# Early priorities of an attention-plus-FFN kernel taken from another replay, and its run-in products removed

## The chip, the cores and the metric

The kernel runs on one core of one Trainium2 chip. The metric is the device time of one execution in microseconds (us). Five engines work from their own instruction queues, each in its program's order: TensorE (PE; its weight loads are listed as PEld), VectorE (DVE), ScalarE (ACT), GpSimd (POOL) and SyncE (SP), which here only issues DMAs.

## The reference

Windowed attention on 8 batches of 8 heads, 576 positions, head size 64, then a Fourier mix over positions and channels, a normalisation and an FFN of 512 to 2048 to 512:

```python
scores = scale * np.matmul(q, k.transpose(0, 1, 3, 2))
# heads 0-3: the last 32 positions; heads 4-7: every 4th of the last 128
scores = np.where(masks[None], scores, -1e9)
attn = softmax(scores)
x = np.matmul(attn, v)                       # heads side by side: (8, 576, 512)
mixed = np.real(fft(fft(x, axis=1), axis=2))
u = x + mixed
un = (u - mean(u)) / np.sqrt(var(u) + 1e-06)
out = u + np.maximum(un @ w_ch1, 0.0) @ w_ch2
```

w_ch1 and w_ch2 come as 64-bit words, which the kernel turns into pairs of 32-bit halves itself.

## The kernel before

**Attention.** Each batch has two kinds of heads (`dil` 1 for the plain ones, 0 for the dilated), and each kind five slots `u`, four whole and one half; so a batch is ten calls of `attend`. A slot is a chain over four engines: 16 small score products on TensorE (8 for the half slot), a mask with a running extreme for each of four head pairs on VectorE (L838), an exponential for each on ScalarE (L844), one or two transpositions on TensorE (L849) and their copy on ScalarE (L854), 16 value products on TensorE (L860), then sums, reciprocals and scaling on VectorE (L877 to L886). The result of batch 0 goes by small DMAs of GpSimd (`dil` 1) and ScalarE (`dil` 0) into the tiles `x`; later batches go through DRAM.

**Behind it** come, per batch, the Fourier mix (L1105 to L1185), the normalisation, and "fills": products with the first six of 16 pieces of the weights (L1358, L1375). From about 540 us on, a main stage of products L1753 and L1863 takes all ten remaining pieces. The weights are loaded by `words_of` (DMA L1259, 512 KB a piece) and unpacked on ScalarE and VectorE (L1261 to L1279).

**What sets the order.** Every operation is given to a planner (`Plan.add`) with an engine, a cost and a priority. `Plan.run` replays the program with these costs, always takes the lowest priority that can start, and the instructions are emitted in that order; on the chip each engine goes through its own list strictly in order, waiting for semaphores. Two tables shift single operations: `MOVED` adds to the priority, `HELD` to the earliest time, each by kind of operation and turn ('k' and 'v' are the loads of keys, queries and values, 's' scores to exponentials, 'p' transpositions to scaling, 'o' stores, 'w' and 'W' weights, 'u' and 'd' the fills, the rest mix and normalisation). Costs and tables act only on the order: nothing on the chip waits for a planned time.

**Buffers.** Scores live in PSUM banks of the names mix and ff, or sc and sd, two of each. Four key tiles kb0 to kb3 serve all batches; kb2 and kb3 hold the keys of the first five slots, kb0 and kb1 those of the next five.

**The run-in.** In the first slot, `scores` issues `N_RUN_IN` = 32 products of a column of zeros (`kb[0]()[:, 0:WIN]`, cleared at L704) before its 16 real ones, into the bank that the real ones then overwrite.

## Time and profile before

| | us |
|---|---|
| median of three runs | 1008.23 (1007.9 to 1010.74) |
| the profiled execution | 1012.46 |
| its span, first to last instruction | 1010.4 |
| TensorE busy | 962.6 (95% of the span) |
| TensorE not busy in 0 to 50 us | 26.0 |
| the same in 50 to 600 us | 13.8 |

The span is what the profile divides up; 2.1 us of the execution lie outside it, and the execution was 4.2 us above the median. TensorE's busy time is a modelled figure, since its matmuls overlap, so a busy TensorE need not be a fast one; idle time is the safer reading.

### The profile page before, as it was taken

How to read it: one execution, taken by the hardware profiler on the slowest of the kernel's cores; microseconds unless marked ns; L12 is line 12 of the kernel's file. 1: busy time of each engine (PE TensorE's matmuls, PEld its weight loads, DVE VectorE, ACT ScalarE, POOL GpSimd, SP SyncE). 2: the span in 40 equal slices, each digit the busy share in tenths (PEclk: the TensorE clock that was granted, in tenths of full speed). 3: DMA queues.
4: the chain of work that ended last, by engine and by line, in shares of the span. 5: the costliest groups of instructions: out<-in, count | busy, mean ns of one | idle time of the engine just before them, and what ended most of it. 6: DMA issues, size and time to landing. Idle time of an engine off the chain costs nothing.

```text
span 1010.4 us, 29386 instructions
## 1 busy us (share of the span) xinstructions
PE 962.6 (95%) x11189; PEld 876.8 (87%) x11189; DVE 820.5 (81%) x2738; ACT 565.6 (56%) x1483; POOL 202.1 (20%) x277
## 2 busy tenths in 40 slices
PE   5499999998999999999999999999999999999997
PEld 4247788887888888998998999999999999999997
DVE  4699776867787889669888599898888888898877
ACT  3465645554456443335455565757576757575663
POOL 3301342635443436500001001000001000000011
PEclk7599999999999999999999999999999999999999
DMA  9767776768785555265888953332313131314031
GB/s 294 231 229 247 246 218 191 231 190 242 232 248 150 180 166 177 63 210 177 289 296 338 307 137 105 64 95 74 115 54 116 53 116 54 117 52 126 1 115 53
DMA packets 110101, 166.63 MB, mean 165 GB/s; under 512 B 13028, under 2 KB 51988, under 8 KB 109962
## 3 DMA queue, kind: packets, MB, share of 16 engines
q1 hardware_dynamic: 106044, 157.42, 50.1%
q0 software_dynamic: 2880, 6.43, 2.1%
q8 instruction: 88, 1.44, 0.6%
q10 hardware_dynamic: 1038, 0.92, 0.3%
q14 instruction: 51, 0.42, 0.1%
HBM read 110.42 MB, written 53.40 MB: 162 GB/s over the span
## 4 chain that ended last, share of the span: by engine, by line
PE 64%; DVE 8%; DMA 4%; ACT 2%; issue 1%; SPq 1%; POOL 0%; DVEq 0%; ACTq 0%; POOLq 0%
PE ff L1753 21%; PE sd L1863 6%; PE ff L1358 6%; PE mix L1863 6%; PE sc L1863 6%; PE ff L1375 5%; PE ff L1863 3%; PE sc L1375 3%; DMA ut<-us 3%; PE sd L1358 3%; PE mix L1170 2%; PE mix L1105 2%; DMA wt<-wst 1%; DVE ut L1506 1%; PE sc L828 1%
## 5 line engine op out<-in xcount | busy, mean ns | idle before, releaser
L1358 PE MATMUL ff<-ut,wa 128*128 128x256 f32 x936 | 128.5, 285 | 1.6 <-DVE h L1367 0.9
L1428 POOL DMA_INDIRECT ut<-us,flip_sb x20 | 24.9, 1246 | 512.1 <-DVE ut L1457 213.2
L1375 PE MATMUL ff<-wa,h 128*128 128x512 f32 x468 | 121.6, 401 | 1.0 <-DVE h L1367 1.0
L1358 PEld LDWEIGHTS ff<-ut,wa 128*128 128x128 f32 x936 | 116.7, 188 | 6.1 <-DVE h L1367 1.7
L844 ACT ACTIVATE pm<-pm,mx 128x64 f32<-128x64 f32 x288 | 79.6, 340 | 53.0 <-DVE mx L838 50.1
L1375 PEld LDWEIGHTS ff<-wa,h 128*128 128x128 f32 x468 | 83.4, 189 | 17.7 <-DVE h L1367 1.4
L1753 PE MATMUL ff<-xb,wa 128*128 128x256 f32 x540 | 75.8, 281 | 0.1
L1753 PE MATMUL ff<-xb,left_w 128*128 128x256 f32 x486 | 69.4, 282 | 1.2 <-ACT sb L1761 0.7
L1753 PEld LDWEIGHTS ff<-xb,wa 128*128 128x128 f32 x540 | 68.4, 188 | 0.4 <-ACT ut L1761 0.4
L1753 PE MATMUL ff<-xb,late_w 128*128 128x256 f32 x486 | 68.8, 280 | 0.0
L1777 ACT ACTIVATE h<-s 128x256 fp32r<-128x256 f32 x134 | 55.4, 417 | 20.6 <-DVE s L1793 16.0
L1753 PEld LDWEIGHTS ff<-xb,left_w 128*128 128x128 f32 x486 | 62.1, 188 | 2.4 <-ACT ut L1761 1.2
L1753 PEld LDWEIGHTS ff<-xb,late_w 128*128 128x128 f32 x486 | 61.8, 188 | 0.3 <-ACT s L1761 0.2
L1365 ACT ACTIVATE h<-ff 128x256 fp32r<-128x256 f32 x78 | 28.4, 382 | 46.7 <-PE ff L1358 46.1
L1753 PE MATMUL ff<-xb,right_w 128*128 128x256 f32 x378 | 52.6, 280 | 0.1
L1761 ACT COPY s<-ff 128x256 f32<-128x256 f32 x90 | 33.5, 372 | 32.4 <-PE ff L1753 31.5
L1753 PEld LDWEIGHTS ff<-xb,right_w 128*128 128x128 f32 x378 | 48.3, 189 | 0.7 <-ACT s L1761 0.3
L1506 DVE STREAM_TRANSPOSE ut<-ut 128x512 f32<-128x512 f32 (+1 forms) x40 | 39.2, 999 | 9.9 <-DMA ut<-us 9.9
L1358 PEld LDWEIGHTS sd<-ut,wa 128*128 128x128 f32 x360 | 44.2, 188 | 2.1 <-DVE h L1367 0.9
L1375 PE MATMUL sc<-wa,h 128*128 128x512 f32 x180 | 44.8, 392 | 0.9 <-ACT h L1365 0.5
L1358 PE MATMUL sd<-ut,wa 128*128 128x256 f32 x360 | 45.2, 280 | 0.1
L854 ACT COPY ptsb<-sc 128x256 f32<-128x256 f32 (+1 forms) x75 | 25.5, 350 | 34.9 <-PE sc L849 34.8
(311 smaller groups left out, 2642.3 us busy)
## 6 DMA issues: line engine op xcount, KB each, us to landing
vt<-in_v_dram SPq DMA_DIRECT2D x64, 260.0 KB
wst<-in_w_dram SPq DMA_DIRECT2D x20, 512.0 KB
wt<-wst SPq DMA_DIRECT2D x40, 256.0 KB
us<-uc SPq DMA_DIRECT2D x36, 257.0 KB
part<-row SPq DMA_DIRECT2D x36, 256.0 KB
ut<-part SPq DMA_DIRECT2D x36, 256.0 KB
kb<-in_k_dram SPq DMA_DIRECT2D x30, 288.0 KB
ut<-in_w_dram SPq DMA_DIRECT2D x12, 512.0 KB
```

Of the source, the lines that this page charges most:

```text
L844: add("ACT", 0.25, lambda i=i: nc.scalar.activation(out=pm()[:, i], in_=pm()[:, i], func=AF.Exp, bias=mx()[:, i:i + 1], scale=-1.0), ((mx, ...
L854: add("ACT", act(n), lambda: nc.scalar.copy(out=pt()[:, 0:n], in_=split[0]()[:, 2 * P:2 * P + n]), (split[0],), (pt,), prio)
L1105: nc.tensor.matmul(ps()[:, :NSP], lhsT=lt, rhs=tab, start=(m == 0 and n == 0), stop=(m == 2 and n == (0 if b == 0 else count - 1)),)
L1358: nc.tensor.matmul(z()[:, :n_tok], lhsT=wf()[:, a, kk], rhs=ut()[:, p, kk], start=(kk == 0 and n == 0), stop=(kk == KT - 1 and n == 2),)
L1365: add("ACT", act(n_tok) - 0.03, lambda: nc.scalar.activation(out=h()[:, 0, :n_tok], in_=z()[:, :n_tok], func=AF.Relu), (z,), ((h, 0),), prio)
L1375: nc.tensor.matmul(acc(), lhsT=h()[:, a, P * s:P * s + P], rhs=wf()[:, p], start=(first and n == 0), stop=(last and n == 2),)
L1428: add("POOL", 1.3, lambda: nc.gpsimd.indirect_dma_start(u(0, C + 2), None, us[idx // 4](), bass.IndirectOffsetOnAxis(ap=flip_sb()[:, 4 * k ...
L1506: nc.vector.transpose(out=o[back], in_=x[:, g])
L1753: nc.tensor.matmul(up_bank()[:, lo:lo + TOK1], lhsT=ap()[:, a, kk], rhs=xb()[:, j, p, kk], start=(start and k == 0), stop=(k == 5), skip_g ...
L1761: add("ACT", act(n), lambda: nc.scalar.copy(out=dst()[:, 0:n], in_=up_bank()[:, 0:n]), (up_bank, held), (dst,), SOON - 1, urgent=True)
L1777: add("ACT", act(TOK1), lambda: nc.scalar.activation(out=ap()[:, 0], in_=src(), func=AF.Relu if relu else AF.Copy), need, (k0,), prio)
L1863: nc.tensor.matmul(acc()[:, TOK1 * half:TOK1 * half + TOK1], lhsT=ap()[:, a, P * half:P * half + P], rhs=wap()[:, q_].rearrange("p k f -> ...
```

## The change

`N_RUN_IN` and the loop that issues the run-in go. The numbers in `MOVED` and `HELD` are replaced by others, found by a replay in which TensorE also waits for its blocks of instructions, which are fetched by DMA behind the loads that are already queued. The computation itself stays as it was. Lines shift by two to seven, so L828 before is L821 now, and so on.

```diff
 N_WARM0, N_WARM1 = 6, 5
-N_RUN_IN = 32
 NXT = 0
...
 MOVED = {
...
-    'k': [19.08, 58.34, 34.6, 63.03, 36.08, 15.45, 40.88, 7.29, 74.69, 49.57, 28.29, 44.49, 25.51, 20.01, 20.91,
...
+    'k': [59.87, 47.84, 49.03, -21.99, 61.44, 42.62, 47.77, 54.19, 103.48, 39.4, 6.16, 32.37, 76.92, 8.06, 16.38,
...
-        run_in = N_RUN_IN if first and u == FIRST_TURNED[0] else 0
-
         def scores():
-            for _ in range(run_in):
-                z = kb[0]()[:, 0:WIN]
-                nc.tensor.matmul(split[0]()[0:WIN, 0:WIN], lhsT=z, rhs=z, start=True, stop=True)
             for j, at, rows, c in tiles():
```

What that does to the order, at three places. First SyncE's list of loads from the start of the program, before and then now (kb are keys, tq queries, the numbers behind a kb tell which tile; kb_175 is kb2, kb_176 is kb3):

```order
L772 DMA kb_176<-in_k_dram 128x256
L694 DMA ident_sb<-in_ident_dram 128x128
L772 DMA kb_174<-in_k_dram 128x576
L787 DMA tq<-in_q_dram 128x256 x2
L772 DMA kb_176<-in_k_dram 128x192
L690 DMA mask_sb<-in_mask_dram 128x320
L772 DMA kb_175<-in_k_dram 128x256
L772 DMA kb_173<-in_k_dram 128x576
L772 DMA kb_176<-in_k_dram 128x128
L772 DMA kb_175<-in_k_dram 128x192
```

```order
L770 DMA kb_175<-in_k_dram 128x192
L688 DMA mask_sb<-in_mask_dram 128x320
L770 DMA kb_173<-in_k_dram 128x576
L770 DMA kb_176<-in_k_dram 128x128
L770 DMA kb_175<-in_k_dram 128x256
L785 DMA tq<-in_q_dram 128x256
L770 DMA kb_174<-in_k_dram 128x576
L785 DMA tq<-in_q_dram 128x256
L770 DMA kb_176<-in_k_dram 128x256
L770 DMA kb_176<-in_k_dram 128x192
```

The first slot needs the first 128 columns of kb2 (loaded from ScalarE's queue) and of kb3 and one tile of queries: they stood up to the tenth DMA (kb_176, 128x128), and now up to the sixth (the first tq).

Second ScalarE's first exponentials (L844, now L837) and copies (L854, now L847), before and then now:

```order
L844 ACTIVATE pm_351<-pm_351,mx_352 128x64 x4
L844 ACTIVATE pm_358<-pm_358,mx_359 128x64 x4
L854 COPY ptsb_379<-mix_279 128x256
L854 COPY ptsb_381<-sc_333 128x256
L844 ACTIVATE pm_450<-pm_450,mx_451 128x64 x4
```

```order
L837 ACTIVATE pm_291<-pm_291,mx_292 128x64 x4
L847 COPY ptsb_335<-mix_273 128x256
L837 ACTIVATE pm_330<-pm_330,mx_331 128x64 x4
L847 COPY ptsb_345<-sc_307 128x256
L837 ACTIVATE pm_418<-pm_418,mx_419 128x64 x4
```

The first slot's copy, which its value products need, no longer stands behind the second slot's exponentials.

Third SyncE's list where the first weights stand, before and then now (in_w is w_ch1 or w_ch2, and ut the tile that its words go to):

```order
L800 DMA vt<-in_v_dram 128x260
L787 DMA tq<-in_q_dram 128x640
L787 DMA tq<-in_q_dram 128x512
L800 DMA vt<-in_v_dram 128x520
L772 DMA kb_175<-in_k_dram 128x576
L1259 DMA ut<-in_w_dram 128x512 x4
L732 DMA row<-in_chn_dram 128x258
```

```order
L798 DMA vt<-in_v_dram 128x260
L785 DMA tq<-in_q_dram 128x640
L798 DMA vt<-in_v_dram 128x520
L785 DMA tq<-in_q_dram 128x512
L770 DMA kb_175<-in_k_dram 128x576
L1252 DMA ut<-in_w_dram 128x512 x4
L785 DMA tq<-in_q_dram 128x640
```

The load of kb2 and the four pieces of weights keep their places; a load of queries has come up behind them. On TensorE the order of slots, transpositions and value products stays nearly that of before (its list is 64 hardware products shorter). One thing moves there: the scores of the third to fifth slots, in before 32 products, then the second slot's value products, then the last 8, now stand in a row of 40.

## Rows read from the trace of the kernel before

**Rows 1.** The page, parts 1 and 2: busy time; 40 slices of 25 us.
```profile
PE 962.6 (95%) x11189; PEld 876.8 (87%) x11189; DVE 820.5 (81%) x2738; ACT 565.6 (56%) x1483; POOL 202.1 (20%) x277
...
PE   5499999998999999999999999999999999999997
...
PEclk7599999999999999999999999999999999999999
```

**Rows 2.** The page, part 3: queue, kind, packets, MB, share of the DMA engines.
```profile
q8 instruction: 88, 1.44, 0.6%
```

**Rows 3.** Stretches of 5 us: busy time and count per engine, TensorE clock, DMA.
```profile
10.00:15.00 5.00, 3.46 (x134) 2.62 (x135) 1.49 (x20) 2.64 (x10) 0.56 (x1) 0.54 1.05 374
15.00:20.00 5.00, 4.03 (x133) 2.47 (x122) 3.63 (x33) 3.46 (x13) 4.03 (x8) 0.50 0.93 298
20.00:25.00 5.00, 3.02 (x158) 2.48 (x157) 3.00 (x31) 2.52 (x10) 3.94 (x9) 0.50 0.98 333
25.00:30.00 5.00, 1.61 (x7) 1.11 (x7) 0.00 (x0) 0.00 (x0) 2.32 (x6) 0.50 0.98 344
```

**Rows 4.** The same view, stretches cut where TensorE waited for "issue".
```profile
15.60:22.90 7.30, 6.49 (x250) 4.76 (x250) 5.30 (x52) 3.98 (x16) 5.87 (x12) 0.50 0.96 314
22.90:28.30 5.40, 0.12 (x7) 0.00 (x0) 0.76 (x12) 2.00 (x9) 2.86 (x6) 0.50 0.97 351
...
28.30:117.40 89.10, 70.90 (x1379) 47.66 (x1380) 80.39 (x387) 52.51 (x150) 18.95 (x30) 0.85 0.73 233
```

**Rows 5.** TensorE's timeline: start, duration, operation [idle before, its releaser].
```profile
3.84 3.46 PE L823 MATMUL mix<-kb 128*32 128x32 f32 x64 [3.84 <-DVE tail_sb L722]
...
10.59 0.28 PE L828 MATMUL mix<-kb,tq 64*32 64x64 f32 x1 [3.01 <-DMA kb<-in_k_dram]
...
14.31 0.31 PE L828 MATMUL mix<-kb,tq 64*32 64x64 f32 x1
...
16.06 0.31 PE L828 MATMUL sc<-kb,tq 64*32 64x64 f32 x1 [0.62 <-issue]
...
20.59 0.31 PE L860 MATMUL mix<-vt,ptsb 64*32 64x65 f32 x1
...
28.39 0.42 PE L828 MATMUL ff<-kb,tq 64*32 64x64 f32 x2 [5.38 <-issue]
...
32.48 0.39 PE L828 MATMUL sc<-kb,tq 64*32 64x64 f32 x2 [1.25 <-DVE xt L886]
...
39.44 0.72 PE L849 MATMUL mix<-ident_sb,pm 128*128 128x128 f32 x2 [5.49 <-ACT pm L844]
```

**Rows 6.** DMA by queue: all in 20 to 26 us (two), instructions in 26 to 28.
```profile
q1 hardware_dynamic: 545, 1.90, 91.0%
q0 software_dynamic: 221, 0.12, 6.6%
...
q8 instruction: 1, 0.02, 3.1%
```

**Rows 7.** SyncE's DMA issues, 14 to 25 us: start, duration, count.
```profile
14.10 0.80 SPq L800 DMA_DIRECT2D vt<-in_v_dram  x1
17.25 0.33 SPq L772 DMA_DIRECT2D kb<-in_k_dram  x1
17.62 3.02 SPq L1259 DMA_DIRECT2D ut<-in_w_dram  x4
...
21.37 2.98 SPq L800 DMA_DIRECT2D vt<-in_v_dram  x4
```

**Rows 8.** ScalarE's own DMA issues in its timeline, two of the groups.
```profile
34.92 1.22 ACTq L935 DMA_DIRECT2D xt<-xt  x2
...
43.75 3.56 ACTq L935 DMA_DIRECT2D x<-xt  x4
```

**Rows 9.** TensorE's waits from 57 us to 1003: total, times, longest (us).
```profile
PE sc L828 <- DVE xt L886: 3.0, 7, 1.0
PE mix L1136 <- issue: 1.4, 1, 1.4
PE sc L860 <- issue: 1.4, 1, 1.4
```

## The prediction

> **What bounds the kernel now.** [...] A later gain of order alone has little room: the largest waits of TensorE from 57 us on are 3.0, 1.4 and 1.4 us in total [rows 9]. The early part decides, and there the timeline [rows 5] shows what a shift is made of. TensorE waits for keys until 10.59, stops for 0.62 us before 16.06 and for 5.38 us before 28.39 with no semaphore that held it ("issue"), and for 5.49 us before 39.44 for an exponential.

> **What the "issue" waits are.** The queue that the profile calls instruction moved 88 packets of 16 KB [rows 2]; TensorE has 22378 matmuls and weight loads [rows 1], so a packet holds 254 of them, 256 with its other instructions. Between the first stop and the second lie 250 + 250 of them, two packets, and between the second and the wait at 117 us 1379 + 1380, which is eleven [rows 4]. So TensorE stops at ends of blocks. No instruction packet moved between 20 and 26 us, while the loads took 91 and 6.6% of the DMA engines; one moved between 26 and 28, and TensorE went on at 28.39 [rows 5, 6]. The block was asked for when TensorE crossed into the block before it. Counted in the program's order (four instructions for an fp32 product, two for a transposition, one for each wait beyond an instruction's first) that is the first value product of the half slot, at 20.59 [rows 5]. Just before, SyncE had queued kb2 (288 KB) and four pieces of weights (512 KB each) from 17.25 to 20.64 [rows 7]: 2.39 MB, or 7.2 us at the 333 GB/s that moved then [rows 3]. From 20.59 to 28.39 are 7.8 us. So the block waited behind the loads, and 2.1 us of those 7.8 had work.

> **The change, part by part.** The sum goes by when the second score product of the dilated half, at 32.48 in before [rows 5], comes in the new order; the list behind it is the same.

> 1. *The run-in.* 64 hardware products, 3.84 to 7.30 [rows 5]. They end before the wait for keys that lasts to 10.59, so taking them away is worth 0. The clock was near half speed with them as well (0.54 over 10 to 15 us, then 0.50) [rows 3], so nothing that they warmed is lost: 0.

> 2. *The start.* The first slot's loads now end after 928 KB instead of 1536 KB, but the second slot's, which stand next on TensorE, still need about 1.6 MB, so they come at about 10.5. The gain is behind them: the first slot's exponentials are done by then and its copy no longer waits for the second slot's. So the value products and the scores of 14.31 [rows 5] can come up to 1.3 us earlier, at 13.0 (two copies and four exponentials off the chain). Bounds 0 and -1.3; I take -1.0, since the block of 40 needs a bank that the first slot gives back.

> 3. *The blocks.* Without the 128 instructions of the run-in every block ends 128 instructions of work later. Counted in the new order the ends fall in the third of 16 value products of the third slot, in the 25th of the 40 scores that opened the dilated half, and in the 12th of the 16 behind them. The first of these blocks is asked for at about 12.9, and the block before took 5.4 us (about 10.7, at the first scores, to 16.06 [rows 5]), so it is there at about 17.8; TensorE arrives at 16.7 and stops for 1.1 us, 0.5 more than in before. At 17.8 it asks for the next. SyncE's wait from 14.90 to 17.25 was for scores that read kb2 [rows 7]; these are done by 14.3 now, so kb2 and the weights are queued from about 15.0 to 18.3. By 17.8 kb2 and three pieces stand there, 1.87 MB, and some 0.8 MB of loads before them, less 0.83 MB moved at 298 GB/s [rows 3]: 1.84 MB, 5.5 us. With the 2.4 us from a packet's start to TensorE (26.0 to 28.39 [rows 5, 6]) the block is there at 25.7 to 26.1. TensorE has work to about 20.3, so it stops for some 5.6 us: the stop of 5.38 us is not removed but comes two microseconds sooner. Bounds: 0, if the block is asked for before the weights are queued, and 8, if kb2, all four and the 0.8 MB stand ahead undrained.

> [...]

> 4. *Up to 32.48.* In before the masks and the exponentials ran during the stop, so 4.1 us lay between 28.39 and 32.48. In the new order the stop comes inside the 40 scores, and VectorE starts with masks of the part that is cut: ten masks and ten exponentials lie behind it, some 5.6 us to the second score product. That gives 26.1 + 5.6 = 31.7, so -0.8 in place of 32.48, between -2.9 and +2.0.

> 5. *From there to 50 us.* The wait that ends at 39.44 is for exponentials behind four DMA issues on ScalarE (the last two end at 36.14), and four more take 3.56 us from 43.75 [rows 8]. They have the same places in the new list, as has the unpacking of weights on VectorE around them: 0, so the -0.8 is carried on. From 50 us TensorE is full, so a shift is kept to the end.

> 6. *Later blocks.* The ends move in the same way against all later work. Two "issue" waits of 1.4 us [rows 9] are what such a stop costs there. They can go, and others can come: between -2.8 and +2.8, and I take 0.

> Sum: 0 - 0.8 + 0 + 0 = -0.8 us. The span would be 1009.6 instead of 1010.4. The profiled execution was 1012.46 and the median of the runs 1008.23; the 0.8 us are taken from the median: **1007.4 us**. A measurement of this kernel can tell about 0.3% from no change, 3.0 us, so this is "no change" in effect.

> **Rivals.** *A, the block is in time.* If TensorE crosses into the block before the weights are queued, the new order has no stop of five microseconds. For it: the change's numbers come from a replay that counts this wait, and TensorE would only have to be there 1.5 to 2.5 us sooner than I reckon. Against it: SyncE is ahead too, because its wait of 2.35 us is gone [rows 7]. The price is the 5.4 us, less what the loads of values behind the weights (21.37 to 24.35 [rows 7]) then hold back: 1002.8 to 1005.0, middle 1003.9. The same time follows if a block need not stand behind the loads at all. [...]

> *B, two stops for one.* The place is the next block, in the 12th of 16 scores, which is asked for when the first stop ends. If that is later than 28.4, it stands behind queries and values queued meanwhile (some 1.36 MB, 4.1 us, and 2.4), is there at 35.1 or later, and the second score product, which starts at 32.48 in before [rows 5], comes 2.6 us late. With 0.6 us of exponentials behind it this is +3.2 or more: 1011.4 to 1013. For it: all four pieces of weights are on the way earlier than before. Against it: 28.4 needs 2.3 us more of queue than 1.84 MB make.

> *C, the forecast*: the stop moves and stays, 1005.2 to 1011.2.

> **How the numbers follow.** C 0.58, A 0.29, B 0.13: the counted places of the blocks speak for C, and the largest doubt is whether 17.8 us is right within two microseconds, more likely early than late. Faster by over 0.3% is A, slower B. The likeliest gives 1007.4; its own range is 1005.2 to 1009.7 by items 2 to 6. The range reaches down to 1002.3, below A's middle by what item 6 can add to it, and up to 1010.8, which leaves out B and a quarter of A.

> **What would show it.** Right: a wait for "issue" of 4 to 7 us on TensorE that ends at 25 to 27 us, inside scores of the 40; one of about 1 us that ends near 17.8; the second scores at 31 to 32.5; TensorE full from about 50 us on. Wrong: no such wait (A), one that ends past 28.4 and another behind it (B), or a gain that comes after 57 us, which no term here has.

## The result, and the profile after

The changed kernel takes 1016.0 us (median of 20 runs, 1012.84 to 1021.26), the kernel before 1010.04 in 20 runs beside them (1007.9 to 1013.24). The ratio is 1.0059, with a 95% interval of 1.0048 to 1.0070: about 6 us slower, where 1007.4 and "no change" were forecast. The profiled execution of after was 1015.23, its span 1013.4, against 1012.46 and 1010.4: the two traces show 3 of the 6 us, since that execution of before lies above its median and that of after below.

The page of after, parts 1 and 2 (TensorE's busy time; 40 slices of 25 us), answers to [rows 1]:

```profile
PE 962.9 (95%) x11125; PEld 875.7 (86%) x11125; DVE 822.1 (81%) x2738; ACT 567.0 (56%) x1483; POOL 205.6 (20%) x277
...
PE   4499999999999999999999999999999999999997
...
PEclk9998999999999999999999999999999999999999
```

At this grain after looks no worse than before: nine tenths or more from 50 us on except the last slice. The first two digits of PEclk can't be compared with those of [rows 1], as shown below. The early part, in TensorE's timeline (start, duration, operation [idle before, its releaser]), answers to [rows 5]:

```profile
13.03 0.31 PE L853 MATMUL mix<-vt,ptsb 64*32 64x65 f32 x1
...
18.91 0.31 PE L853 MATMUL mix<-vt,ptsb 64*32 64x65 f32 x1 [0.92 <-issue]
...
24.95 0.31 PE L821 MATMUL sc<-kb,tq 64*32 64x64 f32 x1 [2.78 <-issue]
...
31.25 0.39 PE L821 MATMUL sc<-kb,tq 64*32 64x64 f32 x2 [1.26 <-DVE xt L879]
...
37.87 0.71 PE L842 MATMUL mix<-ident_sb,pm 128*128 128x128 f32 x2 [5.75 <-ACT pm L837]
```

Two stops at block ends, the second inside the scores of the 40 as counted, but 2.78 us long and not 5.6; the second score product of the dilated half comes at 31.25, 1.2 us sooner than the 32.48 of [rows 5].

The clock was half in the early part, as in [rows 3], although PEclk reads 9 there. The trace of after holds no record of the clock before the rise to full at 54.8 us, and a stretch without a record is counted as full. The products tell it (groups of score products: count | busy, mean ns of one; before in 20 to 50 us, where half is on record, then after in 20 to 50 and in 60 to 80 us):

```profile
L828 PE MATMUL sd<-kb,tq 64*32 64x64 f32 x72 | 3.2, 308 | 0.1
L821 PE MATMUL sd<-kb,tq 64*32 64x64 f32 x72 | 3.4, 309 | 0.0
L821 PE MATMUL sd<-kb,tq 64*32 64x64 f32 x56 | 1.8, 222 | 0.0
```

One product takes 309 ns in after where before takes 308 at half clock, and 222 behind the rise. Later the clock of after fell once more (stretches in us: length, busy time and count of PE, PEld, DVE, ACT, POOL, granted clock as a share of full speed, DMA share, GB/s):

```profile
82.00:90.00 8.00, 7.58 (x121) 6.19 (x121) 6.80 (x38) 3.84 (x12) 0.00 (x0) 0.57 0.82 253
90.00:100.00 10.00, 9.53 (x219) 8.47 (x218) 9.71 (x49) 7.37 (x20) 1.63 (x3) 1.00 0.64 215
```

**Where the time went.** I lined the two traces up by equal amounts of TensorE work, which is an estimate, since the order differs. After is 1.5 us ahead at 57 us, 3.7 ahead at 338 us, 2.0 ahead at 487, 0.8 behind at 596 and 3.2 behind at 677. The gain is there and is lost again between 370 and 680 us. Part of the gain is that both later "issue" waits of 1.4 us [rows 9] are gone from after's trace. The same view in two of these stretches, before and then after:

```profile
370.00:410.00 40.00, 39.32 (x263) 35.79 (x261) 34.35 (x81) 15.25 (x39) 23.84 (x29) 1.00 0.44 136
510.00:620.00 110.00, 108.83 (x811) 102.58 (x810) 89.63 (x207) 64.42 (x155) 6.33 (x3) 1.00 0.77 252
```

```profile
370.00:410.00 40.00, 37.54 (x244) 33.69 (x243) 30.42 (x72) 15.54 (x40) 19.56 (x25) 1.00 0.43 136
510.00:620.00 110.00, 105.75 (x790) 99.83 (x789) 87.08 (x201) 62.59 (x150) 8.40 (x3) 1.00 0.77 247
```

TensorE is idle for 2.46 us of the first stretch instead of 0.68, and for 4.25 of the second instead of 1.17: 4.9 us more, of the 6.9 that it falls back between 338 and 677. Its timeline of after names the waits:

```profile
387.18 4.37 PE L1351 MATMUL ff<-ut,wa 128*128 128x256 f32 x36 [1.78 <-DVE h L1360]
...
522.40 1.68 PE L1351 MATMUL sd<-ut,wa 128*128 128x256 f32 x12 [0.83 <-DVE h L1360]
...
550.86 1.65 PE L1746 MATMUL ff<-xb,right_w 128*128 128x256 f32 x12 [1.63 <-ACT ut L1754]
...
578.23 0.74 PE L1856 MATMUL sd<-late_w,row 128*128 128x256 f32 x4 [0.82 <-DVE row L1777]
```

The tables shift every kind of operation, the fills ('u', 'd'), the weights ('w', 'W') and the main stage's loads too, so the late order is new as well. In the first place VectorE has unpackings of weights (L1307, L1272) ahead of the awaited `h` (its timeline in after):

```profile
381.71 2.73 DVE L1307 TENSOR_TENSOR wst<-wst 128x256 f32<-128x256 f32 x3
384.37 0.41 DVE L1272 TENSOR_TENSOR right_w<-wst,right_w 128x256 fp32r<-128x256 f32 x1
384.70 0.41 DVE L1307 TENSOR_TENSOR wst<-wst 128x256 f32<-128x256 f32 x1
385.04 1.75 DVE L1272 TENSOR_TENSOR right_w<-wst,right_w 128x256 fp32r<-128x256 f32 x5
386.72 0.41 DVE L1360 SCALAR_TENSOR_TENSOR h<-ff,h 128x256 fp32r<-128x256 f32 x1
```

Ten operations in a row stand ahead of `h`, 5.1 us from the first's start to the last's end. In the second place it is ScalarE's copy `ut` that stands behind casts of weights, which wait for their DMA (its timeline in after):

```profile
548.61 0.41 ACT L1333 CAST wst<-wst 128x256 fp32r<-128x256 f32 x1 [3.14 <-DMA wt<-wst]
549.26 0.40 ACT L1333 CAST wst<-wst 128x256 fp32r<-128x256 f32 x1 [0.24 <-DMA wt<-wst]
549.92 0.40 ACT L1333 CAST wst<-wst 128x256 fp32r<-128x256 f32 x1 [0.26 <-DMA wt<-wst]
550.23 0.58 ACT L1754 COPY ut<-ff 128x512 f32<-128x512 f32 x1
```

The theory that I took to the chip: the loss is the late order's, made of these waits. Its rivals: the early part or the missing run-in costs time that the two single traces hide; or these waits are only where a shortage of supply shows, and go next door when removed.

### The profile page after: what moved, and what is told of

The parts are those of the page before. It is cut to its first block, busy times and chain, and to the rows that moved or that the text cites. A ratio compares the mean times of both kernels' runs of the same rounds, so it can differ in the third digit from the quotient of the medians.

```text
span 1013.4 us, 29258 instructions
## 1 busy us (share of the span) xinstructions
PE 962.9 (95%) x11125; PEld 875.7 (86%) x11125; DVE 822.1 (81%) x2738; ACT 567.0 (56%) x1483; POOL 205.6 (20%) x277
## 3 DMA queue, kind: packets, MB, share of 16 engines
q8 instruction: 88, 1.44, 0.6%
## 4 chain that ended last, share of the span: by engine, by line
PE 45%; DVE 11%; DMA 6%; issue 2%; ACT 1%; SPq 1%; DVEq 0%; ACTq 0%
PE ff L1746 19%; PE sd L1856 5%; PE sc L1856 5%; PE mix L1856 5%; DMA ut<-us 4%; PE ff L1856 3%; PE ff L1351 2%; PE ff L1368 2%; DVE ut L1499 1%; DVE wst L1307 1%; PE sd L1351 1%; DVE h L1360 1%; PE sc L1368 1%; SPq L1489 1%; DVE wst L1264 1%
## 5 line engine op out<-in xcount | busy, mean ns | idle before, releaser
L1421 POOL DMA_INDIRECT ut<-us,flip_sb x20 | 28.0, 1400 | 515.3 <-DVE ut L1450 201.9
L837 ACT ACTIVATE pm<-pm,mx 128x64 f32<-128x64 f32 x288 | 79.3, 339 | 49.2 <-DVE mx L831 46.3
L1770 ACT ACTIVATE h<-s 128x256 fp32r<-128x256 f32 x134 | 55.1, 416 | 22.8 <-DVE s L1786 18.3
L847 ACT COPY ptsb<-sc 128x256 f32<-128x256 f32 (+1 forms) x75 | 25.6, 351 | 36.5 <-PE sc L842 36.4
```

The costliest lines, as they stand in the source:

```text
L837: add("ACT", 0.25, lambda i=i: nc.scalar.activation(out=pm()[:, i], in_=pm()[:, i], func=AF.Exp, bias=mx()[:, i:i + 1], scale=-1.0), ((mx, ...
L847: add("ACT", act(n), lambda: nc.scalar.copy(out=pt()[:, 0:n], in_=split[0]()[:, 2 * P:2 * P + n]), (split[0],), (pt,), prio)
L1421: add("POOL", 1.3, lambda: nc.gpsimd.indirect_dma_start(u(0, C + 2), None, us[idx // 4](), bass.IndirectOffsetOnAxis(ap=flip_sb()[:, 4 * k ...
L1770: add("ACT", act(TOK1), lambda: nc.scalar.activation(out=ap()[:, 0], in_=src(), func=AF.Relu if relu else AF.Copy), need, (k0,), prio)
```

## The experiments

The kernels e1 to e11, g2 and g3, but for e3, hold both pairs of tables and replay the plan with each; what is emitted is one order up to a planned time and then what is left of the other, in its order. e3 and e12 are the kernels before and after, e3 without the run-in, and f1 to g1 move single operations in the order of after. A planned time is about 10 us below that of the chip (a cut at 330 lies near 340 us). Every comparison has its own runs of before beside it, whose medians lay between 1010.9 and 1012.7 us; so kernels are compared by their ratio to before, in brackets its 95% interval. These ratios are the ones on record; they are not the quotient of the two medians given with them, from which they differ by up to 1.7 thousandths (e7).

### Early or late, run-in or not

**e1: the new order to 340 us, the old one behind.**

```diff
-N_RUN_IN = 32
+N_RUN_IN = 0
+FIRST_PART, CUT = 0, 330.0
...
-        for o in order:
-            o.fn()
+        (one, at), (two, _) = self.replay(FIRST_PART), self.replay(1 - FIRST_PART)
+        early = {o.num for o in one if at[o.num] < cut}
+        for o in [o for o in one if o.num in early] + [o for o in two if o.num not in early]:
+            o.fn()
```

> The new order up to about 360 us (330 us of the planner's own clock), the old order behind it, no run-in. In the two traces the new order is 4.0 us ahead at 330 us and 3.0 us behind at the end, so 7 us are lost in between, and nothing before. Theory 'late' (the new order of fills and weight unpacking from 375 to 680 us makes TensorE wait): the loss goes and the lead stays, 4 us under before, about 1006. Theory 'run-in' (without the 64 products the clock or the ends of the instruction blocks fall worse): as the changed kernel, about 1016. Theory 'early' (in a typical run the new early order is the slow part): about 1016.

1012.38 against 1012.64: 1.0003 [0.9981, 1.0025]. The early part alone shows neither loss nor gain; with the late order the loss is gone. In its trace the two stretches are as in before:

```profile
370.00:410.00 40.00, 39.33 (x263) 35.81 (x262) 33.17 (x80) 15.13 (x39) 22.74 (x29) 1.00 0.42 136
510.00:620.00 110.00, 108.91 (x813) 102.75 (x812) 89.57 (x208) 64.27 (x154) 7.08 (x3) 1.00 0.79 252
```

**e2: the reverse, with the run-in and the old order to 340 us, the new one behind.**

```diff
-FIRST_PART, CUT = 0, 330.0
+FIRST_PART, CUT = 1, 330.0
```

> The other way round: run-in and old order up to about 360 us, the new order behind it. Theory 'late': 7 us over before, about 1017, with waits of TensorE for VectorE's half of h near 387 us and for ScalarE's copies near 550 and 577 us. Theories 'run-in' and 'early': as before, about 1010.

1017.56: 1.0050 [1.0019, 1.0082], with waits of 1.55 us at 391.59 and of 2.04 at 555.45 at the same two instructions as in after. The late order alone makes nearly the whole loss.

**e3: before without its run-in.**

```diff
-N_RUN_IN = 32
+N_RUN_IN = 0
```

> The kernel before with the run-in alone taken out; its order is the same to the instruction otherwise. Theory 'late': within 2 us of before (1008 to 1012), since the products end before the wait for keys; the ends of the instruction blocks move by 128 instructions, so the stop of 5.4 us before 28.4 us should move. Theory 'run-in': about 1016. Theory 'early': about 1010.

1016.55: 1.0029 [1.0008, 1.0051], so slower, which the prediction's item 1 had at 0. The blocks end elsewhere in the old order too (TensorE's timeline):

```profile
21.82 0.31 PE L860 MATMUL mix<-vt,ptsb 64*32 64x65 f32 x1 [2.59 <-issue]
...
28.13 0.31 PE L828 MATMUL sc<-kb,tq 64*32 64x64 f32 x1 [3.06 <-issue]
...
34.47 0.39 PE L828 MATMUL sc<-kb,tq 64*32 64x64 f32 x2 [1.28 <-DVE xt L886]
```

Stops of 2.59 and 3.06 us stand for 0.62 and 5.38 [rows 5], in sum no more than these, and the second score product is 2 us later. One of these two comes with the first keys, at 11.55 instead of 10.59, which differs from run to run (11.70 in e8, where they stand in the same place of the list). The profiled execution, 1019.14, is the slowest of e3's twelve, and its trace differs in the clock too: it rises to full at 59.3 us (54.7 in before) and falls to half again for 6.8 us at 86.6 and, by a wait of 2.31 us for `h`, at 253.9; the trace of before has no such fall. What makes the loss of e3 is open.

**e4: after with the run-in.**

```diff
-N_RUN_IN = 0
+N_RUN_IN = 32
```

> The changed kernel with the run-in put back; its order is the same to the instruction otherwise. Theory 'late': within 2 us of the changed kernel (1014 to 1018). Theory 'run-in': about 1010. Theory 'early': about 1016.

1015.02: 1.0034 [1.0009, 1.0059]. One stop of 3.96 us, ending at 26.94, stands for after's two, and the late waits stay (1.51 us at 389.26, 1.45 at 551.86). Its interval and that of the change overlap, so the run-in has no worth of its own here that these runs show.

### Which late stretch, and do the weights hold the block

**e5: the change with the old order in the two stretches.**

```diff
+PARTS = (('new', 360.0), ('old', 400.0), ('new', 500.0), ('old', 600.0), ('new', 100000000.0), ('new', 1000000000.0))
```

> The changed kernel with the old order in two stretches only (360 to 400 and 500 to 600 us of the planner's clock, about 10 us later on the chip), the new order everywhere else. In the new order VectorE has ten unpackings in a row ahead of the h that TensorE waits for at 387 us (1.78 us), and ScalarE three casts, which wait for stores of weights, ahead of the copy that gives back TensorE's bank at 550 us (1.63 us); in the old order these stand apart. Theory 'two places' (these and the waits beside them at 522 and 577 us make the loss): the waits go and the time falls by 3.4 to 6 us from 1016, to 1010 to 1012.6. Rival 'symptom' (TensorE is ahead there of loads and stores that set the pace, and what is mended comes back at the next wait): within 1 us of 1016, with other waits of the same sum up to 680 us.

1015.23 against 1010.92: 1.0040 [1.0019, 1.0062]. Both waits are gone from its trace (idle 0.67 and 2.35 us in the two stretches, span 1010.8; that execution, 1012.97, was 2.3 us under e5's median), but the ratio gives back only a third of the loss, less than the sum of the waits, and its interval and that of the change overlap.

**e6 and e8: e1, and before, with the third and fourth piece of weights behind four loads of values on SyncE.** They ask whether a block waits for the bytes queued ahead of it.

```diff
+LATER = (((('w', 2), ('w', 3)), ('v', 9)),)
```

> The new order up to about 340 us and the old one behind it, as in the first experiment, with one change: SyncE issues the third and fourth piece of weights (2 of the first 4, 512 KB each) behind the four loads of values that follow them. Theory 'behind the loads' (a block of TensorE's instructions is fetched only when the loads already queued have passed): 1.05 MB less stand ahead of it, 3.1 us at 335 GB/s, so the stop of 3.4 us at 23 us shrinks to under 1 us; the time falls by up to 3 us if nothing else is late, to 1009 to 1011. Rival 'own cost' (fetching a block at this place costs what it costs): a stop of 3 us stays and the time is that of the first experiment, 1012.

> The kernel before with the same two pieces of weights issued behind the four loads of values, nothing else changed. Theory 'behind the loads': the stop of 5.4 us before 28.4 us shrinks by about 3 us, and the second scores of the dilated half start near 29.5 instead of 32.5 us; the time falls by 1 to 3 us. Rival 'own cost': the stop stays over 5 us and the time within 1 us of before.

e6 1013.77: 1.0017 [0.9994, 1.0039]. e8 1010.42: 0.9989 [0.9968, 1.0011]. The stop in e1, e6 and e8, in that order:

```profile
26.32 0.31 PE L941 MATMUL sc<-kb,tq 64*32 64x64 f32 x1 [3.07 <-issue]
```

```profile
25.38 0.31 PE L963 MATMUL sc<-kb,tq 64*32 64x64 f32 x1 [3.88 <-issue]
```

```profile
27.14 0.42 PE L963 MATMUL ff<-kb,tq 64*32 64x64 f32 x2 [3.35 <-issue]
```

With two pieces (1.05 MB) behind the loads of values, e6's stop did not shrink (3.07 to 3.88), while e8's did (5.38 to 3.35). When TensorE crossed into the block before, the queue held 1.74, 2.25, 1.77, 1.57 and 1.25 MB in before, after, e1, e6 and e8 (bytes that SyncE had begun to issue, less those whose packets had started); so e6, which crosses 1.7 us sooner than e1, had only 0.2 MB less ahead. From the crossing to the packet were 5.45, 3.79, 3.81, 4.38 and 2.66 us, in which 1.67, 1.44, 1.36, 1.27 and 0.85 MB left that queue. The waits do not follow the bytes, and in after the packet moved with 0.8 MB still waiting. So a queue that holds the block strictly behind all bytes ahead of it, as the prediction and the replay have it, is refuted; what does set the wait stays open. And 2 us off the largest early stop show no gain clear of noise in e8's ratio, whose interval still holds one of that size.

**e7: e1 with the run-in.**

```diff
-N_RUN_IN = 0
+N_RUN_IN = 32
```

> The first experiment's order with the run-in of 32 products put back, so that the ends of the instruction blocks lie 128 instructions earlier. Theory 'ends of blocks' (the run-in only shifts the ends, which in this order cost 1.6 + 3.4 us without it and 4.2 us in one stop with it): 1 to 2.5 us less than without the run-in, 1010 to 1011.5. Rival 'nothing in it': the first experiment's 1012.4 within 1 us. Rival 'clock' (the run-in lets the clock fall to half from 10 to 55 us, which costs): over 1013.

1013.13: 1.0005 [0.9984, 1.0027], as e1. With the new early order the run-in is worth nothing that these runs show, with the old one its removal cost 2.9 thousandths (e3).

### The stretches again, by exclusion

**e9: the new order to 610 us. e10: new to 340 us and in the two stretches, old elsewhere. e11: new to 370 and from 410 to 510 us, old elsewhere. e12: the changed kernel once more, for its ratio in the same comparison.**

```diff
+PARTS = (('new', 600.0), ('old', 100000000.0), ('old', 1000000000.0))
...
+PARTS = (('new', 330.0), ('old', 360.0), ('new', 400.0), ('old', 500.0), ('new', 600.0), ('old', 100000000.0), ('old', 1000000000.0))
...
+PARTS = (('new', 360.0), ('old', 400.0), ('new', 500.0), ('old', 100000000.0), ('old', 1000000000.0))
```

> The new order up to about 610 us (600 of the planner's clock), the old order behind it, no run-in. The new order lost 5.6 thousandths behind 340 us; the old order in the two stretches gave back only about 2 of these in the median, though in its one trace the loss was gone. Theory 'two stretches' (the loss lies between 370 and 610 us): as the changed kernel, 5 to 6 us over before. Theory 'end' (the rest lies behind 610 us): 2 to 4 us over before.

> The new order up to 340 us, and again from 370 to 410 and from 510 to 610 us; the old order in all the rest, no run-in. Theory 'two stretches': they alone cost what the changed kernel costs, 5 to 6 us over before, with the waits of 1.8 us near 387 and near 550 us in the trace. Theory 'end', or a loss spread over other places: 1 to 3 us over before.

> The new order up to 370 us and from 410 to 510 us, the old order in the rest, no run-in; beside the kernel with the old order in the two stretches, the part behind 610 us is old too. Theory 'two stretches': within 1.5 us of before. Theory 'end': within 1.5 us of before as well, but then 3 to 4 us under the kernel whose end was new. A loss between 410 and 510 us, the only part behind 370 us that is new here: 3 us or more over before.

> The changed kernel itself once more, beside these on the same chip: 5 to 7 us over before by its first 20 runs (5.9 thousandths, 4.8 to 7.0). It also gives a second trace: theory 'order' has the waits near 387 and near 550 us again at 1.8 and 1.6 us, and a chance event would not come twice.

Against 1011.92: e9 1018.29, 1.0065 [1.0043, 1.0086]; e10 1019.59, 1.0073 [1.0045, 1.0101]; e11 1013.9, 1.0024 [1.0004, 1.0043]; e12 1016.45, 1.0058 [1.0033, 1.0083]. e12 confirms the change's ratio, and its trace has the two waits again, 1.89 us for `h` at 389.34 and 1.87 for `ut` at 553.03. e10 is e1 with the new order in two stretches of some 40 and 100 us, and with these the whole loss is back; what comes behind 610 us has no part in it that shows. But e5, without them, keeps two thirds of it: the stretches are enough for the loss, and not shown to be all of it. Its stretches:

```profile
370.00:410.00 40.00, 37.87 (x250) 34.25 (x249) 34.22 (x80) 14.69 (x37) 23.57 (x30) 1.00 0.43 136
510.00:620.00 110.00, 106.49 (x785) 100.25 (x784) 88.05 (x204) 64.61 (x154) 7.31 (x2) 1.00 0.79 253
```

TensorE's idle time in them (length less PE busy, us), for before, the change and the kernels so far that mix the orders or, as e4, have the new one throughout:

| | early part | 370 to 410 | 510 to 620 | ratio to before |
|---|---|---|---|---|
| before | old | 0.68 | 1.17 | 1 |
| e1 | new | 0.67, old order | 1.09, old order | 1.0003 |
| e11 | new | 0.68, old | 1.66, old | 1.0024 |
| e4 | new, run-in | 2.18, new | 1.98, new | 1.0034 |
| e5 | new | 0.67, old | 2.35, old | 1.0040 |
| e2 | old | 2.23, new | 4.04, new | 1.0050 |
| e12 | new | 2.56, new | 4.25, new | 1.0058 |
| after | new | 2.46, new | 4.25, new | 1.0059 |
| e9 | new | 2.95, new | 3.77, new | 1.0065 |
| e10 | new | 2.13, new | 3.51, new | 1.0073 |

The old order in the stretches goes with the lower ratios, the new one with the higher, and e4 and e5 cross. e5 and e11 have the old order in the stretches and pieces of the new one around them; their intervals reach down to 1.0019 and 1.0004, so a seam or a remainder may cost something there that was not found. No run prices a seam by itself, so e10's 1.0073 can hold the price of its seams as well.

### Is it the operations ahead of the awaited one

**f1: the change with the three casts behind the copy `ut`. f2: with the unpackings (the ten, and one behind the first `h`) and four casts spread behind the next four `h`. f3: both.** Numbers are those of the operations: each is emitted behind its mark, as far as its users allow.

```diff
+BEHIND = ((4432, 4493), (4435, 4499), (4438, 4504))
...
+BEHIND = ((4113, 3099), (4115, 3099), (4114, 3099), (4118, 3105), (4116, 3105), (4120, 3105), (4124, 3105), (4126, 3111), (4122, 3111), (4128, 3117), ...
```

> The changed kernel, and on ScalarE the three casts ahead of the copy at 550 us moved behind it, each behind one later operation, with their partners on VectorE; every other list is word for word the same. Theory 'list': the wait of TensorE of 1.6 to 1.9 us for that copy goes and does not come back, so the time falls by 1.5 to 2 us from 1016. Rival 'store' (what the casts wait for, the stores of weights, is what is late, and TensorE meets it at its next use): the wait stands at a place a little later, 1016.

> The changed kernel, and the ten unpackings in a row on VectorE ahead of the h near 387 us spread behind this h and the next three, as are the four casts on ScalarE that stand ahead of the activation for it; every other list is the same. Theory 'list': the wait of 1.8 us goes, 1.5 to 2 us less than 1016. Rival 'VectorE is full there': the wait goes to the next h, 1016.

> Both of these moves at once, nothing else. Theory 'list': 3.3 to 3.9 us less than 1016, and what is left over before (about 2 us) is made of the smaller waits near 522, 577 and 609 us. Rivals as in the other two: 1016.

Against 1012.74: f1 1019.66, 1.0076 [1.0048, 1.0103]; f2 1019.07, 1.0064 [1.0041, 1.0088]; f3 1019.48, 1.0079 [1.0052, 1.0106]. None gains. f1's wait at 550 is gone, and another stands 17 us behind it (TensorE's timeline, then ScalarE's):

```profile
568.19 0.98 PE L1896 MATMUL ff<-xb,left_w 128*128 128x256 f32 x6 [2.39 <-ACT sb L1904]
```

```profile
565.90 0.42 ACT L1920 ACTIVATE row<-s 128x256 fp32r<-128x256 f32 x1 [2.78 <-DMA part<-row]
567.25 0.42 ACT L1920 ACTIVATE row<-ut 128x256 fp32r<-128x256 f32 x1 [0.93 <-DMA part<-row]
567.57 0.57 ACT L1904 COPY sb<-ff 128x512 f32<-128x512 f32 x1
```

The copy `sb` now stands behind two operations that wait for stores of rows, which SyncE has among its loads of weights. In f3 the wait at 387 falls into 0.90 and 0.33:

```profile
393.64 1.65 PE L1501 MATMUL ff<-ut,wa 128*128 128x256 f32 x12 [0.90 <-DVE h L1510]
395.62 3.70 PE L1518 MATMUL ff<-wa,h 128*128 128x512 f32 x15 [0.33 <-DVE h L1510]
```

and the stretch is still idle for 2.06 us (2.46 in after). So the operations right ahead are not the cause by themselves. What differs is how much VectorE has to do while TensorE runs one row of 60 products; its groups in that row, in before (386.7 to 394.5 us) and then in after (382.3 to 391.6; line, engine, operation, count | busy, mean ns | idle):

```profile
L1314 DVE TENSOR_TENSOR wst<-wst 128x256 f32<-128x256 f32 x3 | 1.2, 409 | 0.0
L1279 DVE TENSOR_TENSOR right_w<-wst,right_w 128x256 fp32r<-128x256 f32 x5 | 1.8, 410 | 0.0
```

```profile
L1307 DVE TENSOR_TENSOR wst<-wst 128x256 f32<-128x256 f32 x4 | 3.1, 825 | 0.0
L1272 DVE TENSOR_TENSOR right_w<-wst,right_w 128x256 fp32r<-128x256 f32 x7 | 2.6, 411 | 0.0
```

Eight unpackings, 3.0 us, in before; eleven, 5.7 us, in after, of which three took 0.91 us each. f3, which spread them, still has nine in that row. That fits the first stretch; that it is the cause is argued from these counts, which lie close together, and not shown by an edit.

**g1: f1 with the stores of rows ahead of the weights on SyncE. g2: the change with the old order in the first stretch alone. g3: in the second alone.**

```diff
-BEHIND = ((4432, 4493), (4435, 4499), (4438, 4504))
+BEHIND = ((4432, 4493), (4435, 4499), (4438, 4504), (4075, 4074), (4077, 4076), (4442, 4076), (4443, 4076), (4444, 4076))
...
+PARTS = (('new', 360.0), ('old', 400.0), ('new', 100000000.0), ('new', 1000000000.0))
...
+PARTS = (('new', 500.0), ('old', 600.0), ('new', 100000000.0), ('new', 1000000000.0))
```

> The kernel with the three casts behind the copy, and on SyncE the two stores of rows (part) ahead of the last store of weights and of the first three loads of late_w; all other lists the same. With the casts moved the wait of 1.6 us at 550 us had gone, but a wait of 2.4 us for ScalarE's copy of sb stood near 568, behind an activation that waited 2.5 us for the store of a row, which stood in SyncE's list behind stores and loads of weights that were themselves waiting. Theory 'SyncE's list': that wait goes and the time is 2 us under that kernel's 1.0076 of before, near 1.0055. Rival 'supply' (the weights' stores, later by the moved casts, hold TensorE somewhere anyway): another wait of 1 to 2.5 us up to 620 us, 1.007 or more.

> The changed kernel with the old order between 370 and 410 us only. If the two stretches add up, this gives back what the traces show there, 1.8 to 2 us: 3.5 to 4.5 us over before. If TensorE waits in the second stretch for something that comes at its own time, the lead is lost there: 5 us or more over before.

> The changed kernel with the old order between 510 and 610 us only. If the two stretches add up, 2 to 3 us over before (the first stretch's 2 us stay, the 3 to 4 us of the second go). If the loss hangs on the first stretch (what comes late there comes late in the second as well): 5 us or more over before.

Against 1012.23: g1 1021.21, 1.0092 [1.0059, 1.0124]; g2 1017.08, 1.0052 [1.0034, 1.0069]; g3 1017.72, 1.0057 [1.0037, 1.0078]. g1's wait at 568 is gone, and a new one stands near 580 (its waits from 560 to 620 us: total, times, longest):

```profile
PE sd L2006 <- ACT row L1920: 2.0, 1, 2.0
```

f1 and then g1 moved the second stretch's wait to the next operation that needs weights or rows. So it is not the place of one operation; that the supply through SyncE is late there fits both, but no run changed the supply alone, and it stays open. TensorE is idle for 0.68 and 2.53 us in g2's two stretches, and for 2.99 and 2.57 in g3's: the old order mends the first stretch wholly, the second in part, and the new one left the second at 2.53 this time. Yet both ratios barely differ from after's 1.0059 (e12: 1.0058), and g2's traced waits are near those of e5 at 1.0040: the two stretches do not simply add, and the waits of one trace do not price a kernel within 2 us.

## Why the prediction was wrong

**What held.** The steps to 57 us, by after's rows above. *Item 2:* the scores that began at 14.31 came at 13.46, -0.85 for the -1.0 taken, with the first value product at 13.03 (13.88 in before). *Item 3:* two stops at the counted places, of 0.92 us (forecast 1.1) ending at 18.91 (17.8), and one that ends at 24.95, a microsecond before the 25.7 to 26.1 forecast. Its length was mis-sized: 2.78 and not 5.6, because TensorE arrived two microseconds later than reckoned and the packet came sooner than the queue allows: 3.79 us from the crossing, for the 5.5 reckoned from 1.84 MB, with 2.25 MB there. The rule behind item 3, that a block waits behind all bytes queued, is refuted by that. It had looked right in before because the 2.39 MB were taken as all still there, when 1.74 were. By the prediction's own sign, a wait of 4 to 7 us, the stop failed. *Item 4:* 31.25, so -1.2 for the forecast -0.8. That is near by luck: the stop ended a microsecond early, and 6.3 us instead of 5.6 lay behind it. *Item 5, to 50 us:* 37.87 against 39.44, carried on, 1.5 us ahead at 57.

**What failed.** First, "A later gain of order alone has little room", from which I concluded that "The early part decides". [rows 9] shows the waits that a new late order could take away; it sets no bound on those that one can add. The change moves numbers of every kind of operation, and items 5 and 6 priced the late part by ends of blocks alone, between -2.8 and +2.8, taken as 0. Waits for `h`, the copy `ut` and `row`, 4.9 us more idle time in two stretches, which no item had, came instead. With the prediction's own -0.8 they give +4.1, and from 1008.23 that would have been 1012.3, outside its range: the term was left out, not mis-sized. That the late order makes the loss is shown by e1 and e2; that these waits are all of it is not (e5).

Second, "From 50 us TensorE is full, so a shift is kept to the end". A slice of 25 us at nine tenths can hold 2.5 us of waits, and of that size is what came. The lead of 1.5 us, 3.7 at 338 us in the trace, was spent there. And e1, which has the early part without the late one, shows none of this lead in its ratio (1.0003 [0.9981, 1.0025], an interval in which the forecast's -0.8 us lies as well), so single traces overrate it.

Third, *item 1*: taking the run-in away was put at 0 and costs 3 us in the old order (e3). The block ends move there by 128 instructions, which the prediction counted in the new order only, but the stops of e3 sum to no more than before's, and its trace has falls of the clock that before's has not; the cause stays open. In the new order the run-in is worth nothing that e1 and e7 can tell.

Fourth, the base: 1008.23 was a median of three runs, and 20 runs gave 1010.04. That shifts the forecast by 1.8 us, and does not mend its sign. The range does not follow from the items either: items 4 and 6 alone reach +4.8, so 1013.0 where it ends at 1010.8, and A's middle less item 6's 2.8 is 1001.1 where it begins at 1002.3. In *B* 28.4 + 4.1 + 2.4 is 34.9 and not 35.1, and 2.4 of the 7.8 us before 28.39 had work and not 2.1. None of this reaches the 6 us that came.

**The rivals.** *B* had the sign and the wrong place: its second stop near 35 us did not come. *A* did not come either, though the stop halved; what a shorter stop is worth no run tells clear of noise (e8, where 2 us of the old stop went: 0.9989 [0.9968, 1.0011]). *Not settled:* what makes the second stretch late, why e5, g2 and g3 give back less than their waits, what e3 loses by, and what sets a block's wait. No kernel tried was faster than before beyond its interval; e8 comes nearest (0.9989).

## What to carry to other kernels

A table of priorities that is searched anew changes the whole order, whatever part it was searched for: compare each engine's list where TensorE is nearly full, and look at how many operations of other work stand between two that it waits for, before saying that only the aimed-at part moves. Waits in a full stretch bound what a new order can gain there, never what it can lose; for the loss, the awaited engine's work per row of products is a first thing to count. A gain of one or two microseconds in one trace is within what the next execution moves (before's 20 runs lie between 1007.9 and 1013.24), so aim a table at a part by emitting the old order behind it, as e1 does.

## What the runs showed of the hardware

**The clock.** In all 20 traces full clock came between 52.7 and 59.3 us (54.7 in before, 54.8 in after, 59.3 in e3). In the six with the old early order or the run-in half clock is on record from 27 us at the latest up to that rise (in before from 10.4 us, with full clock for 3.4 us behind the run-in). In the 14 with the new early order and no run-in the rise is the first record. In after the score products took 309 ns in the mean from 10 to 50 us, as before's at half clock, and 222 from 60 to 80; single ones took 0.31 us in e1 at 26.32 and in e6 at 25.38 (above), where e1 has 0.21 to 0.24 at 240. So it was half in these three too, and they won no clock over before in the early part. The mean clock listed for a run counts time without a record as full, so those of the two groups can't be compared. Inside one group they can: of after's 20 runs the six at 0.998 or more have a median of 1014.6 us, the seven at 0.995 or less 1017.1. Falls behind the rise are part of the spread of single runs; they hardly make the loss, since the median run of e1 has 0.997 and of after 0.996.

The fall of after at 82 to 90 us, in the rows above, stands in 10 of those 14 traces and in e3 and e8. The longest wait of TensorE ahead of it in after, from 74 us on, was 0.73 us. It lasted 6.8 us, in which by the 309 and 222 ns some 2 us of work are lost, an estimate. Other falls stand at the end of a wait: of the 15 waits of TensorE of 2.0 us or more behind 57 us in the 20 traces, nine have one, six have none, and waits of 1.53 to 1.82 us have one in e2, e7 and g2. In g3 it stands behind 2.31 us for `h` (TensorE's timeline, then stretches):

```profile
392.69 5.97 PE L1493 MATMUL ff<-ut,wa 128*128 128x256 f32 x36 [2.31 <-DVE h L1502]
```

```profile
388.00:394.00 6.00, 3.69 (x32) 3.49 (x32) 6.00 (x16) 2.18 (x6) 1.67 (x2) 1.00 0.45 175
394.00:398.00 4.00, 4.00 (x23) 4.00 (x23) 2.76 (x11) 0.77 (x2) 1.23 (x2) 0.57 0.27 79
398.00:402.00 4.00, 4.00 (x22) 3.40 (x22) 3.17 (x9) 2.02 (x5) 1.97 (x2) 1.00 0.64 164
```

The same 36 products take 4.37 us in after, behind 1.78 us, and 5.97 here: the fall costs 1.6 us on top of the wait. e9's wait of 2.27 at the same place had no such fall.

**Unpackings of two speeds.** L1307 took 0.91 us each at 381.7 in after, while GpSimd ran additions of its own from 381.7 to 384.2, and 0.41 at 384.70. In before one took 0.41 at 385.81 beside such additions, so their neighbourhood alone does not set it. There, as at 386.75 and 387.68, it started 0.02 to 0.04 us ahead of GpSimd's addition, which then took 0.96 to 0.99 us, where the three ahead of the first took 0.72 to 0.74. In after GpSimd's had started first, at 381.68, and took 0.73 us. What sets the two speeds was not shown.
